# Scaling s by rows only in its two halves, with the row scales made for two tiles at once

## The chip, the cores and the metric

The kernel runs on one core of a Trainium2 chip. The metric is the time of one execution on the device in microseconds (us); lower is better. The core has five engines with a queue of instructions each, executed in order: PE multiplies matrices into PSUM, DVE (VectorE) does reductions and elementwise work, ACT (ScalarE) does functions and scaled copies, POOL (GpSimd) does elementwise work in SBUF, and SP issues the DMAs. They wait for each other by semaphores.

## The reference, cut to what matters

Two steps follow each other. The first is a causal attention over 7 taps with weights from a softmax over the taps; it turns `x` (8, 4160, 192) into 33280 rows of 192. The second works on these rows:

```python
h = x @ w_in                                   # 192 -> 1024
e = np.exp(h - max(h));  sm = e / (sum(e) + 1e-9)
solu = h * sm
ln = (solu - mean(solu)) / np.sqrt(var(solu) + 1e-6) * g_ln
return ln @ w_out                              # 1024 -> 192
```

max, sum, mean and var go over the 1024 columns of a row.

## The kernel before, in words

The 33280 rows lie as 128 partitions of 260 rows each. A *tile* t is one row of every partition, so there are 260 tiles of 128 rows, and tile after tile goes through the same stages.

*Attention, on POOL.* Four tiles make a group (the first two groups have two), 66 groups in all. `attention` multiplies x by the tap weights (L133), adds three taps to three (L139) and adds again into `half` (L141); `half` has two buffers. A reduction on DVE, the *final sum* (`last_sum`, L379, called `fin` in the order), makes the rows `a` of the group from it; `a` has three buffers. The tap weights come from a softmax in seven steps t0 to t6, for 16 tiles at once, spread over DVE, ACT and POOL.

*First product.* PE transposes two tiles of `a` (`xT`, L396). ACT takes the high part (L404); the low part comes from PE and ACT (L411, L418) or from DVE (L426, L427), taking turns by pairs. Ten matmuls make `h`, 128 x 1024, in PSUM (`mm1`, L440). There are three buffers `h`.

*Between the products*, by tile: DVE takes the negated maximum of a row (`max`, L454). Two small steps make the row scale: `bound` (`vb`, L458) takes the larger of |maximum| and 0.5, and `row_scale` (`vr`, L463) its reciprocal, SIGMA. ACT makes e = exp(h - max) and its row sum Z (`exp`, L467). DVE overwrites h with h x SIGMA x e and sums it (`solu`, L473). ACT sums the squares of its deviation (`sq`, L479). The result s is then split into two float16 numbers: the high half on ACT (`hi`, L486), with a scale of 2^14, and the low half, what is missing to it, on DVE (`lo`, L490). A DMA from SP transposes both (`tr`, L498).

*Second product.* 24 matmuls make `po` (`mm2`, L542), which has one buffer. ACT scales each row of it by OUT into `ot` (`out`, L553), and SP stores four tiles at once (`od`, L556).

*The statistics chain* (`scales`) makes OUT for four tiles at once from Z, SIGMA and the sums in eight steps f0 to f7, four small ones on ACT (L513, L517, L521 with L523, L529) and four reductions on DVE (all L510).

*The order.* Nothing is scheduled at run time: `issue_order` (L615) writes the order of every engine's queue before the program is built. It is a planner: each step has an engine, an assumed cost in ns and a list of steps that it follows; the engine that is free first takes, among its steps that are ready, the one with the smallest sum of tile number and an urgency from the table `URGENCY`. The assumed costs fix where steps of different engines come to stand relative to each other, thus also after which row maximum a final sum (which needs POOL) stands in DVE's queue.

Of the kernel before, what the change touches and what calls it, by code (L numbers as in the profile page):

```python
# [26 lines left out]
def tile_kernel(ctx: ExitStack, tc: tile.TileContext, x, weight_gen, w_in, w_out, g_ln, out):  # L27
    nc = tc.nc
    P = 128
# [14 lines left out]
    D2 = D - P  # L44
    FH = FF // 2

    const = ctx.enter_context(tc.tile_pool(name="const", bufs=1))
# [113 lines left out]
    nc.vector.memset(ones, 1.0 / FF)  # L161
    sq = const.tile([P, 4], F32, name="sq")

    minus = const.tile([P, 2, P], F32R, name="minus")
# [133 lines left out]
    def prepare_second(step, half=None):  # L298
# [11 lines left out]
        elif step == 6:  # L310
# [8 lines left out]
            )  # L319
            nc.vector.tensor_scalar_add(kinv, k, (127 - 73 + 1) << 23)  # L320
            nc.vector.tensor_scalar(k, k, -1, (127 + 73) << 23, op0=ALU.mult, op1=ALU.add)
        elif step == 4:
            k = second["k"] = small.tile([P, 1], F32, name="k", bufs=1)
            nc.scalar.copy(k, second["total"][:, 9:10])
            for n, factor in enumerate((-0.5, 1.5)):
                nc.scalar.activation(
                    newton[:, n : n + 1], second["total"][:, 10:11], AF.Copy, scale=factor
                )
        elif step == 7:
            js = slice(half * NJ // 2, (half + 1) * NJ // 2)  # L330
            nc.scalar.activation(
                w2_hl[:, js, 0, :], second["centred", half], AF.Copy, scale=second["k"]
            )
# [111 lines left out]

    ZE, SIGMA, Q, E, Y, V, Y2, R, OUT, M, Z, U, L, T, NMAX, HALF, BOUND = range(17)
    stats = const.tile([P, 6, TG, 17], F32, name="stats")
    nc.gpsimd.memset(stats[:, :, :, HALF], 0.5)
# [7 lines left out]

    def bound(t):
        nc.vector.tensor_reduce(  # L458
            stat(t, BOUND), stat(t, NMAX, 2), axis=AX.X, op=ALU.max, apply_absolute_value=True
        )  # L460

    def row_scale(t):
        nc.vector.reciprocal(stat(t, SIGMA), stat(t, BOUND))  # L463

# [6 lines left out]
    def solu(t):  # L471
        h, e = h_of[t], e_of[t]
        nc.vector.scalar_tensor_tensor(  # L473
            out=h, in0=h, scalar=stat(t, SIGMA), in1=e, op0=ALU.mult, op1=ALU.mult, accum_out=stat(t, M)
        )
# [8 lines left out]
    def high_half(t):  # L484
        hl = hl_of[t] = big.tile([P, 2, FF], F16, name="hl", bufs=3)
        nc.scalar.activation(hl[:, 0, :], h_of[t], AF.Copy, scale=2.0**14)  # L486

    def low_half(t):
        hl = hl_of[t]
        nc.vector.scalar_tensor_tensor(  # L490
            out=hl[:, 1, :], in0=h_of[t], scalar=2.0**14, in1=hl[:, 0, :],
            op0=ALU.mult, op1=ALU.subtract,
# [9 lines left out]
    def scales(t, step):  # L502
# [9 lines left out]
        if step == 0:  # L512
            nc.scalar.activation(of(ZE), of(Z), AF.Copy, bias=1e-9)  # L513
        elif step == 1:
            reduce(U, ZE, 2, ALU.mult)
        elif step == 2:
            nc.scalar.activation(of(E), of(U), AF.Square, scale=1e-3 * FF**1.5)  # L517
        elif step == 3:
            reduce(V, Q, 2, ALU.add)
        elif step == 4:  # L520
            nc.scalar.activation(of(L), of(V), AF.Ln)  # L521

            nc.scalar.activation(  # L523
                rows[:, :, Y : Y2 + 1 : 2], of(L).broadcast_to([P, n, 2]), AF.Exp, scale=-0.5
            )
        elif step == 5:
            reduce(T, Y, 3, ALU.mult)
        elif step == 6:
            nc.scalar.activation(  # L529
                of(R), of(T), AF.Identity, bias=newton[:, 1:2], scale=newton[:, :1]  # L530
            )
        elif step == 7:
            reduce(OUT, Y2, 2, ALU.mult)

# [52 lines left out]
    for n in range(LOADS):  # L587
        ops[f"lx{n}"] = at_chunk(load_x, n)
    for n in range(8):
        ops[f"f{n}"] = at(scales, n)  # L590
# [10 lines left out]
URGENCY = dict(  # L601
    a00=-20.7, a01=134, a02=5.2, a03=110.1, a04=63.2, a10=74.6, a11=-12, a12=-31.8, a13=49,
    a14=11.9, attA=47.9, attB=50.1, b0=42.1, b1=-15.1, b2=-35.2, b3=27.5, b4=95.3, b5=-24,
    c00=77.1, c01=-3.7, c02=-1.7, c10=81, c11=-48.9, c12=36.9, c20=-140.1, c21=-124.9, c22=47.5,
    c30=6.5, c31=125.3, c32=-83, dup=30.2, exp=67.3, f0=-40, f1=13.8, f2=-1.8, f3=0.8, f4=-12.5,
    f5=-133.2, f6=-27.2, f7=-17.9, fin=8.6, hi=4.9, lo=8.3, lw=8.7, lx0=-110.7, lx1=6.4, lx2=1.5,
    lx3=145.6, max=15.7, mm1=1.2, mm2=7.8, od=19.4, out=9, p30=99.5, p31=-21.1, p4=127.3,
    p5=-119.6, p6=38.8, p70=-21.5, p71=-29.7, p80=-68.4, p81=171.2, q00=149.9, q01=10.2, q02=126.8,
    q10=-10, q11=46.5, q12=-64.7, q20=-100.6, q21=-62, q22=138.4, q30=76.2, q31=-32, q32=-4,
    solu=-94.1, sq=153.2, t0=134, t1=-73, t2=29.5, t3=16, t4=-3.4, t5=130, t6=12.7, tr=-67.4,  # L610
    vb=-7.4, vr=-127.6, xT=-0.2, xhi=-140.5, xld=-4, xlo=-48.1, xn=-53.3,
)


def issue_order(run, starts, group, stat_group, loads):  # L615
# [37 lines left out]
    once("b5", SP, 0, "b4")  # L653
    for half in "01":
        once("p3" + half, DVE, 868, "q31", "mm1" if half == "0" else "q30", *(["p30"] if half == "1" else []))
    once("p5", PE, 220, "q02", "q12", "q22", "q32", "q31")
# [69 lines left out]
    for t in range(run):  # L726
        after = [("b5", 0), ("a04", 0), ("a14", 0)] if t == 0 else []
        if t < 3:

            after += ([("q10", 0), ("c30", 0)], [("p31", 0), ("sq", 0), ("lo", 0)], [("p80", 0)])[t]  # L730
        if t == 3:
            after.append(("p81", 0))
        add("mm1", t, PE, 2250, low_of(t), ("sq", t - 3), ("lo", t - 3), *after)
        add("max", t, DVE, 1131, ("mm1", t), ("exp", t - 4))
        add("vb", t, DVE, 70, ("max", t), ("f7", stats_of[t - 24] if t >= 24 else -1))
        add("vr", t, DVE, 70, ("vb", t))
        add("exp", t, ACT, 1091, ("max", t), ("sq", t - 2))
        add("solu", t, DVE, 1210, ("exp", t), ("vr", t))
        add("sq", t, ACT, 1091, ("solu", t))
        add("hi", t, ACT, 904, ("solu", t), ("tr", t - 3))  # L740
        add("lo", t, DVE, 1135, ("hi", t))
# [4 lines left out]
        else:  # L746
            after.append(("out", t - 1))
        add("mm2", t, PE, 2280, ("tr", t), *after)
        add("out", t, ACT, 304, ("mm2", t), ("f7", stats_of[t]), ("od", t // 4 * 4 - 5))
        if n := stat_group(t):  # L750
            tiles = range(t - n + 1, t + 1)
            add("f0", t, ACT, 200, *(("exp", u) for u in tiles))
            add("f1", t, DVE, 70, ("f0", t), *(("vr", u) for u in tiles))
            add("f2", t, ACT, 200, ("f1", t))
            add("f3", t, DVE, 70, ("f2", t), *(("sq", u) for u in tiles))
            add("f4", t, ACT, 400, ("f3", t))
            add("f5", t, DVE, 70, ("f4", t))
            add("f6", t, ACT, 200, ("f5", t), ("p4", 0))
            add("f7", t, DVE, 70, ("f6", t))
        if t % 4 == 3:  # L760
# [98 lines left out]
```

## Time and profile before

| what | before |
|---|---|
| median of 3 runs | 1400.43 us (1398.85 to 1400.59) |
| profiled execution | 1399.32 us |
| its span | 1397.5 us, so 1.8 us lie around it |
| mean granted clock of PE | 0.987 |
| HBM read, written | 46.19 MB, 25.56 MB |

The profile page gives each engine's busy time and its share of the span. A group of instructions is one line of the kernel on one engine: its name reads output<-inputs, then shapes, count, busy us, mean ns of one, and the idle time ahead of them with what ended it. A line of the waits reads: who, for whom, us in total, times, longest. In a line of the windows stand the stretch, its length, and then busy us and the count in brackets, for all five engines and PE's weight loads, or for those instructions alone that were asked for; the last three numbers are the granted clock, the DMA share and GB/s. A line of the timeline begins with its start and its duration in us.

### The profile page before, as it was taken

What the parts mean: (1) busy time and instruction counts of PE and PEld (TensorE: products, weight loads), DVE (VectorE), ACT (ScalarE), POOL (GpSimd) and SP (SyncE); (2) the same over time, 40 slices, a digit from 0 to 9 for tenths busy, and PEclk for the clock granted to TensorE, in tenths of its full rate; (3) what the DMA queues carried; (4) which work ended last, traced back from release to release, by engine and by line L of the source; (5) the groups of instructions that cost most, each with busy time, mean ns of one, the idle gap of its engine ahead of it and who ended that gap; (6) DMA issues with size and microseconds to landing.
All of it is one profiled execution on the core that took longest, in us unless ns stands there. A gap on an engine that the chain in (4) does not pass through costs nothing.

```text
span 1397.5 us, 25636 instructions
## 1 busy us (share of the span) xinstructions
PE 1252.0 (90%) x9508; PEld 1074.0 (77%) x9508; DVE 1249.2 (89%) x2135; ACT 1130.3 (81%) x2231; POOL 1247.8 (89%) x243
## 2 busy tenths in 40 slices
PE   0398999989999998989999999989999899999997
PEld 0277878878788787878888787878878788888786
DVE  2988999989999998899899999989999999999984
ACT  1577888878888887888788888878887888888885
POOL 1999999999999999999999999999999999998000
PEclk9999999999999999999999999999999999999999
DMA  3567769687878877786959777686969687656665
GB/s 94 168 146 177 152 131 200 135 182 129 184 129 173 168 145 159 132 203 123 199 111 191 142 149 171 131 183 125 209 112 207 117 184 144 129 118 129 128 123 121
DMA packets 565878, 211.43 MB, mean 151 GB/s; under 512 B 544457, under 2 KB 545913, under 8 KB 565752
## 3 DMA queue, kind: packets, MB, share of 16 engines
q1 hardware_dynamic: 565752, 209.78, 72.7%
q8 instruction: 75, 1.23, 0.4%
q14 instruction: 51, 0.42, 0.1%
HBM read 46.19 MB, written 25.56 MB: 51 GB/s over the span
## 4 chain that ended last, share of the span: by engine, by line
POOL 50%; DVE 18%; issue 13%; ACT 13%; PE 3%; DMA 2%; SPq 1%; POOLq 0%; DVEq 0%; ACTq 0%
POOL pr L133 26%; POOL pr L139 14%; POOL half L141 6%; DVE h L473 5%; ACT e L479 4%; ACT hl L486 4%; DVE stats L454 3%; DVE hl L490 3%; DVE a L379 2%; ACT e L467 2%; PE h L440 2%; POOL wt L114 2%; POOL wt L126 2%; DMA raw_a<-in_moe_w_in_dram 1%; PE po L542 1%
## 5 line engine op out<-in xcount | busy, mean ns | idle before, releaser
L133 POOL TENSOR_TENSOR pr<-xt,wt 128x5376 f32<-128x5376 f32 (+1 forms) x66 | 631.6, 9569 | 22.5 <-DMA xt<-zeros 19.8
L542 PE MATMUL po<-w_hl,hlT 128*128 128x192 f16 x6192 | 560.5, 248 | 27.7 <-ACT ot L553 26.8
L542 PEld LDWEIGHTS <-hlT 128*128 128x128 f16 x6240 | 519.0, 98 | 72.8 <-issue 70.0
L473 DVE SCALAR_TENSOR_TENSOR h<-h,stats,e 128x1024 f32<-128x1024 f32 x260 | 335.0, 1288 | 23.0 <-ACT e L467 11.2
L490 DVE SCALAR_TENSOR_TENSOR hl<-h,hl 128x1024 f16<-128x1024 f32 x260 | 316.8, 1220 | 34.0 <-ACT e L479 28.3
L486 ACT ACTIVATE hl<-h 128x1024 f16<-128x1024 f32 x260 | 267.5, 1029 | 96.5 <-DVE stats L510 53.2
L139 POOL TENSOR_TENSOR pr<-pr 128x2304 f32<-128x2304 f32 (+1 forms) x66 | 333.2, 5048 | 5.2
L454 DVE TENSOR_REDUCE stats<-h 128x1 f32<-128x1024 f32 x260 | 316.4, 1217 | 10.1 <-PE h L440 9.6
L467 ACT ACTIVATE e<-h,stats 128x1024 f32<-128x1024 f32 x260 | 292.7, 1126 | 34.2 <-DVE stats L454 30.0
L479 ACT ACTIVATE e<-h,stats 128x1024 f32<-128x1024 f32 x260 | 292.3, 1126 | 15.4 <-DVE hl L490 15.3
L440 PE MATMUL h<-wa_hi,x_hi 128*128 128x512 f32 x520 | 226.0, 435 | 40.2 <-ACT e L479 17.7
L141 POOL TENSOR_TENSOR half<-pr 128x1536 f32<-128x1536 f32 (+1 forms) x66 | 226.1, 3426 | 5.2
L440 PE MATMUL h<-wa_lo,x_hi 128*128 128x512 f32 x520 | 207.1, 398 | 0.0
L440 PE MATMUL h<-wa_hi,x_lo 128*128 128x512 f32 x520 | 206.6, 397 | 0.0
L440 PEld LDWEIGHTS h<-wa_hi,x_hi 128*128 128x128 f32 x520 | 99.3, 191 | 64.2 <-ACT e L479 23.2
L396 PE MATMUL pa<-ident,a 128*128 128x128 f32 x520 | 80.4, 277 | 46.4 <-DVE a L379 44.0
L379 DVE TENSOR_REDUCE a<-half 128x768 f32<-128x1536 f32 (+1 forms) x66 | 116.6, 1766 | 1.2 <-POOL half L141 1.2
L440 PEld LDWEIGHTS h<-wa_hi,x_lo 128*128 128x128 f32 x520 | 99.1, 191 | 23.3 <-ACT x_lo L418 0.2
L553 ACT ACTIVATE ot<-po,stats 128x192 f32<-128x192 f32 x258 | 111.0, 430 | 4.9 <-PE po L542 4.8
L396 PEld LDWEIGHTS pa<-ident,a 128*128 128x128 f32 x520 | 64.9, 143 | 62.3 <-DVE a L379 44.0
L440 PEld LDWEIGHTS h<-wa_lo,x_hi 128*128 128x128 f32 x520 | 99.8, 192 | 12.3
L440 PE MATMUL h<-wb_lo,x_lo 128*128 128x512 f32 x260 | 103.7, 399 | 0.0
(84 smaller groups left out, 1308.4 us busy)
## 6 DMA issues: line engine op xcount, KB each, us to landing
out_dram<-ot SPq DMA_DIRECT2D x65, 384.0 KB, 3.2
xt<-in_x_dram SPq DMA_DIRECT2D x30, 576.0 KB, 4.8
xt<-in_x_dram SPq DMA_DIRECT2D x30, 480.0 KB, 4.3
wt<-in_weight_gen_dram SPq DMA_DIRECT2D x15, 448.0 KB, 4.8
hlT<-hl SPq DMA_TRANSPOSE x260, 4.5
raw<-in_moe_w_out_dram SPq DMA_DIRECT2D x1, 1536.0 KB, 9.3
xt<-in_x_dram SPq DMA_DIRECT2D x3, 384.0 KB, 5.6
raw_a<-in_moe_w_in_dram SPq DMA_DIRECT2D x2, 512.0 KB, 11.4
```

What stands on the lines that cost most here:

```text
L133: nc.gpsimd.tensor_tensor(out=window(pr, 0, [(TG * D, K), (HG, n * H), (1, HG)]), in0=window(xt, t * D, [(D, K), (HG, n * H), (1, HG)]), i ...
L139: nc.gpsimd.tensor_tensor(out=pr[:, :3], in0=pr[:, :3], in1=pr[:, 3:6], op=ALU.add)
L141: nc.gpsimd.tensor_tensor(out=half, in0=window(pr, 0, [(2 * TG * D, 2), (D, n), (1, D)]), in1=window(pr, TG * D, [(5 * TG * D, 2), (D, n), ...
L396: nc.tensor.matmul(pa[:, n, i, :], a[:, (t + i) % TG, n * P : (n + 1) * P], ident, is_transpose=True, start=i == n == 0, stop=i == n == 1,)
L440: nc.tensor.matmul(h[:, fs], lhs, rhs[:, fs], start=n == 0, stop=n == len(terms) - 1)
L454: nc.vector.tensor_reduce(stat(t, NMAX), h_of[t], axis=AX.X, op=ALU.max, negate=True)
L467: nc.scalar.activation(e, h_of[t], AF.Exp, bias=stat(t, NMAX), accum_out=stat(t, Z))
L473: nc.vector.scalar_tensor_tensor(out=h, in0=h, scalar=stat(t, SIGMA), in1=e, op0=ALU.mult, op1=ALU.mult, accum_out=stat(t, M))
L479: nc.scalar.activation(e_of.pop(t), h_of[t], AF.Square, bias=stat(t, M), scale=-float(FF), accum_out=stat(t, Q),)
L486: nc.scalar.activation(hl[:, 0, :], h_of[t], AF.Copy, scale=2.0**14)
L490: nc.vector.scalar_tensor_tensor(out=hl[:, 1, :], in0=h_of[t], scalar=2.0**14, in1=hl[:, 0, :], op0=ALU.mult, op1=ALU.subtract,)
L542: nc.tensor.matmul(po[:, :D], hlT[:, half * NJ + j, :], w2_hl[:, j, w, :], start=n == 0, stop=n == len(terms) - 1,)
```

## The change

`solu` no longer multiplies by the row scale: it takes the constant 2^14 in its place, so it needs neither `vb` nor `vr`. The row scale SIGMA comes in where s is split: it replaces the constant 2^14 in `hi` and `lo`. `vb` and `vr` are done for two tiles at once, behind the maximum of the odd one, so that `hi` of an even tile follows the maximum of the next tile. The statistics chain drops SIGMA from its product of Z and SIGMA: six steps f0 to f5 are left, three on ACT (the first a square with a constant column `tiny` as its bias) and three on DVE, and the last of them multiplies SIGMA in. Constants (`UNIT`) keep the numbers in range.

In the planner the costs of the two products change from 2250 and 2280 to 2450 and 2200, a few steps of the start have other predecessors, and every urgency is new. The softmax steps of four chunks change places with groups in POOL's queue among the groups before tile 36; from there on POOL's queue is the same.

```diff
     def bound(t):
+        rows = stats[:, t // TG % 6, t % TG - 1 : t % TG + 1, :]
         nc.vector.tensor_reduce(
-            stat(t, BOUND), stat(t, NMAX, 2), axis=AX.X, op=ALU.max, apply_absolute_value=True
+            rows[:, :, BOUND], rows[:, :, NMAX : HALF + 1], axis=AX.X, op=ALU.max,
+            apply_absolute_value=True,
         )
     def row_scale(t):
-        nc.vector.reciprocal(stat(t, SIGMA), stat(t, BOUND))
+        rows = stats[:, t // TG % 6, t % TG - 1 : t % TG + 1, :]
+        nc.vector.reciprocal(rows[:, :, SIGMA], rows[:, :, BOUND])
...
     def solu(t):
-            out=h, in0=h, scalar=stat(t, SIGMA), in1=e, op0=ALU.mult, op1=ALU.mult, accum_out=stat(t, M)
+            out=h, in0=h, scalar=S_UNIT, in1=e, op0=ALU.mult, op1=ALU.mult, accum_out=stat(t, M)
...
-        nc.scalar.activation(hl[:, 0, :], h_of[t], AF.Copy, scale=2.0**14)
+        nc.scalar.activation(hl[:, 0, :], h_of[t], AF.Copy, scale=stat(t, SIGMA))
...
-            out=hl[:, 1, :], in0=h_of[t], scalar=2.0**14, in1=hl[:, 0, :],
+            out=hl[:, 1, :], in0=h_of[t], scalar=stat(t, SIGMA), in1=hl[:, 0, :],
...
         if step == 0:
-            nc.scalar.activation(of(ZE), of(Z), AF.Copy, bias=1e-9)
+            nc.scalar.activation(of(E), of(Z), AF.Square, bias=tiny, scale=1e-3 * UNIT)
         elif step == 1:
-            reduce(U, ZE, 2, ALU.mult)
-        elif step == 2:
-            nc.scalar.activation(of(E), of(U), AF.Square, scale=1e-3 * FF**1.5)
-        elif step == 3:
             reduce(V, Q, 2, ALU.add)
...
-            reduce(OUT, Y2, 2, ALU.mult)
+            reduce(OUT, Y2, 3, ALU.mult)
...
 URGENCY = dict(
-    a00=-20.7, a01=134, a02=5.2, a03=110.1, a04=63.2, a10=74.6, a11=-12, a12=-31.8, a13=49,
+    a00=-72.1, a01=-8.5, a02=6.8, a03=10.7, a04=5.4, a10=158.8, a11=116.1, a12=5.7, a13=11.5,
...
-        add("mm1", t, PE, 2250, low_of(t), ("sq", t - 3), ("lo", t - 3), *after)
+        add("mm1", t, PE, 2450, low_of(t), ("sq", t - 3), ("lo", t - 3), *after)
...
-        add("vb", t, DVE, 70, ("max", t), ("f7", stats_of[t - 24] if t >= 24 else -1))
-        add("vr", t, DVE, 70, ("vb", t))
+        if t % 2:
+            add("vb", t, DVE, 70, ("max", t), ("max", t - 1), ("f5", stats_of[t - 24] if t >= 24 else -1))
+            add("vr", t, DVE, 70, ("vb", t))
...
-        add("solu", t, DVE, 1210, ("exp", t), ("vr", t))
+        add("solu", t, DVE, 1210, ("exp", t))
-        add("hi", t, ACT, 904, ("solu", t), ("tr", t - 3))
+        add("hi", t, ACT, 904, ("solu", t), ("vr", t | 1), ("tr", t - 3))
...
-        add("mm2", t, PE, 2280, ("tr", t), *after)
+        add("mm2", t, PE, 2200, ("tr", t), *after)
```

First place: DVE's queue around the 45th final sum, that of tiles 172 to 175 (`a`<-`half`). Before, `h_9914` belongs to tile 162 and `h_9988` to tile 163 (L454 is the maximum, L473 the product, L490 the low half, L458 and L463 the row scale):

```order
L454 TENSOR_REDUCE stats_131<-h_9914 128x1
L458 TENSOR_REDUCE stats_131<-stats_131 128x1
L463 RECIPROCAL stats_131<-stats_131 128x1
L490 SCALAR_TENSOR_TENSOR hl_9936<-h_9863,hl_9936 128x1024
L379 TENSOR_REDUCE a_9984<-half_9761 128x4x192
L473 SCALAR_TENSOR_TENSOR h_9914,stats_131<-h_9914,stats_131,e_9975 128x1024
L454 TENSOR_REDUCE stats_131<-h_9988 128x1
```

In the changed kernel, whose lines have other numbers (L459 maximum, L481 product, L498 low half, L464 and L471 the row scale, L384 the final sum), `h_9456` belongs to tile 158 and `h_9523` to tile 159:

```order
L459 TENSOR_REDUCE stats_133<-h_9456 128x1
L498 SCALAR_TENSOR_TENSOR hl_9475<-h_9403,stats_133,hl_9475 128x1024
L481 SCALAR_TENSOR_TENSOR h_9456,stats_133<-h_9456,e_9515 128x1024
L384 TENSOR_REDUCE a_9539<-half_9304 128x4x192
L459 TENSOR_REDUCE stats_133<-h_9523 128x1
L431 TENSOR_TENSOR x_lo_9571<-pa_9518,x_hi_9567 128x256
L432 TENSOR_TENSOR x_hi_9567<-pa_9518,x_hi_9567 64x256
L464 TENSOR_REDUCE stats_133<-stats_133 128x2
L471 RECIPROCAL stats_133<-stats_133 128x2
```

The same final sum stands behind the maximum of tile 162 before (163 maxima ahead of it) and behind that of tile 158 now (159 ahead). At the 29th final sum (tiles 108 to 111) it is 102 and 99, at the last (256 to 259) 245 and 243. The row scale stands once behind the maximum of an odd tile.

Second place: ACT's queue at tiles 250 and 251. Before (L467 exponential, L486 high half, L479 squares, L553 scaled output), `h_15160` is tile 250 and `h_15222` tile 251:

```order
L486 ACTIVATE hl_15237<-h_15160 128x1024
L479 ACTIVATE e_15212,stats_131<-h_15160,stats_131 128x1024
L467 ACTIVATE e_15267,stats_131<-h_15222,stats_131 128x1024
L553 ACTIVATE ot_15235<-po_15239,stats_131 128x192
L513 ACTIVATE stats_131<-stats_131 128x4
L486 ACTIVATE hl_15288<-h_15222 128x1024
```

In the changed kernel (L475 exponential, L494 high half, L487 squares, L557 scaled output) `h_14817` is tile 250 and `h_14878` tile 251:

```order
L487 ACTIVATE e_14872,stats_133<-h_14817,stats_133 128x1024
L409 CAST x_hi_14917<-pa_14838 128x512
L475 ACTIVATE e_14922,stats_133<-h_14878,stats_133 128x1024
L557 ACTIVATE ot_14828<-po_14891,stats_133 128x192
L494 ACTIVATE hl_14933<-h_14817,stats_133 128x1024
L521 ACTIVATE stats_133<-stats_133,tiny_100 128x4
L494 ACTIVATE hl_14948<-h_14878,stats_133 128x1024
```

The high half of tile 250 stood ahead of its squares and of the exponential of tile 251; now it stands behind both, and the high halves of the two tiles follow each other.

More of the change, by code (lines that the diff above doesn't have):

```diff
@@ L443, in first_product @@
         h_of[t] = h
-    ZE, SIGMA, Q, E, Y, V, Y2, R, OUT, M, Z, U, L, T, NMAX, HALF, BOUND = range(17)
-    stats = const.tile([P, 6, TG, 17], F32, name="stats")
+    Q, E, Y, V, Y2, R, BOUND, OUT, M, Z, L, T, NMAX, HALF, SIGMA = range(15)
+    stats = const.tile([P, 6, TG, 15], F32, name="stats")
     nc.gpsimd.memset(stats[:, :, :, HALF], 0.5)
@@ L588, in tile_kernel @@
         ops[f"lx{n}"] = at_chunk(load_x, n)
-    for n in range(8):
+    for n in range(6):
         ops[f"f{n}"] = at(scales, n)
@@ L653, in issue_order @@
     once("b5", SP, 0, "b4")
-    for half in "01":
-        once("p3" + half, DVE, 868, "q31", "mm1" if half == "0" else "q30", *(["p30"] if half == "1" else []))
+    add("p30", 0, DVE, 868, ("q31", 0), ("mm1", 1))
+    once("p31", DVE, 868, "p30", "sq", "lo")
     once("p5", PE, 220, "q02", "q12", "q22", "q32", "q31")
@@ L752, in issue_order @@
             add("f0", t, ACT, 200, *(("exp", u) for u in tiles))
[L753 to L759, printed above, removed]
+            add("f1", t, DVE, 70, ("f0", t), *(("sq", u) for u in tiles))
+            add("f2", t, ACT, 400, ("f1", t))
+            add("f3", t, DVE, 70, ("f2", t))
+            add("f4", t, ACT, 200, ("f3", t), ("p4", 0))
+            add("f5", t, DVE, 70, ("f4", t), *(("vr", u | 1) for u in tiles))
         if t % 4 == 3:
```

45 lines of the change are left out of this document (24 added, 21 removed).

## Prediction

> **What bounds the kernel now.** I read the page first, for who is busy; then the busy time by stretches, then the waits; and last I counted instructions at chosen moments, because no share told enough.
>
> ```profile
> PE 1252.0 (90%) x9508; PEld 1074.0 (77%) x9508; DVE 1249.2 (89%) x2135; ACT 1130.3 (81%) x2231; POOL 1247.8 (89%) x243
> ```
>
>
> Three engines are near 90% of the span. By stretches (length, then busy us and count of PE, PEld, DVE, ACT, POOL) they differ:
>
> ```profile
> 1000.00:1200.00 200.00, 187.84 (x1441) 161.66 (x1439) 184.48 (x315) 168.41 (x333) 197.80 (x37) 0.99 0.76 151
> 1306.00:1376.00 70.00, 66.54 (x516) 57.28 (x516) 59.96 (x107) 56.76 (x112) 0.00 (x0) 1.00 0.62 126
> ```
>
> In the middle POOL is busy 98.9% (197.80 of 200), PE 94%, DVE 92%, ACT 84%. POOL hardly ever waits:
>
> ```profile
> POOL pr L133 <- DMA xt<-zeros: 19.8, 1, 19.8
> POOL wt L126 <- DVE wy L124: 7.0, 1, 7.0
> ```
>
> Those are its two large waits, one time each, before the first group is under way. So POOL walks through its 66 groups of tiles at its own pace and the main loop (product, maximum, exponential, product on DVE, halves, second product) follows. POOL's steps, with the end of the 45th group (tiles 172 to 175) and of the last (256 to 259):
>
> ```profile
> 886.58 3.45 POOL L141 TENSOR_TENSOR half<-pr 128x1536 f32<-128x1536 f32 x1
> 1285.77 3.46 POOL L141 TENSOR_TENSOR half<-pr 128x1536 f32<-128x1536 f32 x1
> ```
>
> They end at 886.58 + 3.45 = 890.03 and 1285.77 + 3.46 = 1289.23. How far is the main loop then? I counted POOL's last steps (L141, one a group, first fence) and the row maxima (L454 on DVE, one a tile, second fence) that had begun by such moments, the count in brackets:
>
> ```profile
> 0.00:580.60 580.60, 97.55 (x29) 0.98 0.73 154
> 0.00:890.00 890.00, 153.02 (x45) 0.98 0.75 155
> ```
>
> ```profile
> 0.00:580.60 580.60, 124.01 (x102) 0.98 0.73 154
> 0.00:890.00 890.00, 198.27 (x163) 0.98 0.75 155
> 0.00:1289.20 1289.20, 294.46 (x242) 0.99 0.74 153
> 890.00:1289.20 399.20, 96.19 (x79) 0.99 0.73 149
> ```
>
> 163 maxima by 890.0 and 242 by 1289.2: 79 in 399.2 us, a pace of 5.05 us a tile. The run ends 1397.5 - 1289.2 = 108.3 us after POOL does, with 18 maxima still to come. So the end is set by the main loop, which has fallen far behind POOL, and not by POOL itself.
>
> The place where the two meet is the final sum of a group (L379, on DVE), which reads what POOL wrote:
>
> ```profile
> L379 DVE TENSOR_REDUCE a<-half 128x768 f32<-128x1536 f32 (+1 forms) x66 | 116.6, 1766 | 1.2 <-POOL half L141 1.2
> ```
>
> DVE waited for POOL there 1.2 us in the whole run: before, each of these sums stands in DVE's order just behind the moment at which POOL is ready.
>
> **The change part by part: the order.** This is the largest term, and no line of the new arithmetic shows it. The planner's costs and urgencies are new, and so is the place of L379 among the maxima. In the listing of the kernel before, 163 maxima stand ahead of the 45th final sum; in the changed one 159. DVE executes in order, so in the changed kernel the 160th maximum can't begin before POOL has ended that group. POOL's own order and work are the same from tile 36 on (softmax steps change places among the groups before; that sum is the same), so this moment stays 890.0, where the kernel before was at 163. Everything behind the waiting sum on DVE is held: the next product, maximum and low half; behind them ACT (exponential, halves) and PE, which needs an h buffer back. The changed kernel is thus four tiles, at 5.05 us some 20 us, later at this point, whatever its engines could do. It is no single accident: ahead of the 29th final sum, whose group POOL ended at 580.6, stand 99 maxima, against the 102 that had begun.
>
> From there it has to catch up. The last final sum stands behind 243 maxima (245 before), so at 1289.2 it can have begun 243 at most, one more than before. That takes 84 tiles in 399.2 us, 4.75 us each. Slower than that, POOL no longer holds it and its own pace decides:
>
> maxima begun at 1289.2 = 159 + 399.2 / pace; time lost = (242 - that number) x pace; given back in the last 18 tiles = 18 x (5.05 - pace).
>
> **The change part by part: the pace.** DVE loses work:
>
> ```profile
> L463 DVE RECIPROCAL stats<-stats 128x1 f32<-128x1 f32 x260 | 41.7, 161 | 5.7
> L458 DVE TENSOR_REDUCE stats<-stats 128x1 f32<-128x2 f32 x260 | 38.3, 147 | 2.2
> L510 DVE TENSOR_REDUCE stats<-stats 128x4 f32<-128x8 f32 (+3 forms) x268 | 42.1, 157 | 13.4 <-ACT e L479 7.9 <-ACT stats L529 4.5 <-ACT stats L523 0.7
> L473 DVE SCALAR_TENSOR_TENSOR h<-h,stats,e 128x1024 f32<-128x1024 f32 x260 | 335.0, 1288 | 23.0 <-ACT e L467 11.2 <-ACT x_lo L418 0.5 <-ACT ot L553 0.5
> L490 DVE SCALAR_TENSOR_TENSOR hl<-h,hl 128x1024 f16<-128x1024 f32 x260 | 316.8, 1220 | 34.0 <-ACT e L479 28.3 <-ACT hl L486 3.8 <-ACT k L324 0.7
> ```
>
> Bound and reciprocal once for two tiles: 130 x (147 + 161) = 40.0 us less; two elements in place of one cost at most what L510 shows for four (157), so no more than 1.3 us comes back. The chain's four reductions become three: 67 x 157 = 10.5 us. Together some 50 us, 0.19 us a tile. The product (L473) loses its per-row operand and the low half (L490) gains one; if that is the 68 ns between their rows, the two cancel.
>
> ACT gains and loses:
>
> ```profile
> L486 ACT ACTIVATE hl<-h 128x1024 f16<-128x1024 f32 x260 | 267.5, 1029 | 96.5 <-DVE stats L510 53.2 <-DVE h L473 40.7 <-DVE stats L458 1.1
> L467 ACT ACTIVATE e<-h,stats 128x1024 f32<-128x1024 f32 x260 | 292.7, 1126 | 34.2 <-DVE stats L454 30.0 <-DVE stats L463 1.8 <-DVE stats L510 1.0
> L331 ACT ACTIVATE w_hl<-h,k 128x768 f16<-128x768 f32 x2 | 1.7, 897 | 0.0
> L513 ACT ACTIVATE stats<-stats 128x4 f32<-128x4 f32 (+1 forms) x67 | 15.9, 237 | 0.5
> L517 ACT ACTIVATE stats<-stats 128x4 f32<-128x4 f32 (+1 forms) x67 | 14.1, 211 | 1.9 <-DVE stats L510 1.8
> ```
>
> The high half now scales by a row's number. L467, as wide and with a per-row bias, is 97 ns longer than L486. L331 has a per-row scale on 768 columns: between L517 (211 at 4) and L486 (1029 at 1024) a plain one would take about 824, so the operand costs 73. 260 x (73 to 97) = 19 to 25 us more; L513 goes, 15.9 us less; the square gains a per-row bias, 67 x (0 to 97) = 0 to 6.5 us. Net 3 to 16 us, 0.01 to 0.06 us a tile, on an engine that is idle 16% of the time and waits 96.5 us ahead of this very step: nothing, while DVE is later than ACT. If that cover goes, it is 0.06.
>
> The change adds a wait: the high half of an even tile now needs the maximum of the next one, since their scales are made together. Queued behind it on ACT stand the partner's high half and its squares; DVE's low half waits for it, and PE for the h buffer. In ACT's new order it stands behind the partner's exponential, which needs the same maximum, so I cost it at nothing; if the three h buffers are too few for that, the pace suffers (a rival below). On SP the x loads stand four transposes earlier than before in the middle of the run; with the main loop four tiles later the moment is the same, so nothing.
>
> How much of DVE's 0.19 reaches the pace? Bounds: all of it, 4.86; or nothing, 5.05, if PE sets it. What PE waits for:
>
> ```profile
> PE po L542 <- ACT ot L553: 26.8, 39, 3.2
> PE pa L411 <- ACT x_hi L404: 19.9, 24, 3.5
> PE h L440 <- ACT e L479: 17.7, 19, 3.2
> ```
>
> Its largest waits in the loop are for ACT; these three make 64 us. And the stretch 1306 to 1376 is an experiment that the trace made itself: no final sums, no softmax, POOL silent, DVE down to 86% (59.96 of 70). The maxima there:
>
> ```profile
> L454 DVE TENSOR_REDUCE stats<-h 128x1 f32<-128x1024 f32 x14 | 17.1, 1219 | 1.2 <-PE h L440 1.2
> ```
>
> 14 in 70 us, 5.0 each: DVE was freed of 116.6 / 260 = 0.45 us a tile and the pace gained 0.05, with PE at 95%. By this row 0.19 would bring some 0.02; the other end is 0.19. PE is busy 94% of 5.05, or 4.74; each step below 5.05 must come out of its 0.31 of idle time. I take 0.10, in the middle, since PE's waits for ACT hang on the order too, and that is new everywhere: pace 4.95. Then 159 + 399.2 / 4.95 = 239.65; lost 2.35 x 4.95 = 11.6; given back 18 x 0.10 = 1.8. Span 1397.5 + 11.6 - 1.8 = 1407.3. The profiled execution took 1399.3 for its span of 1397.5, so 1.8 lies around it; it is 1.1 under the median of 1400.4. Forecast: 1409 us, slower.
>
> One page weighs the engines otherwise. The Trainium skill (Perfetto Trace Analysis, Identifying the Most-Contended Engine) holds that matmul busy time is a bad measure of PE and that its weight loads should be read in its place. In the stretch from 1000 to 1200 these are 161.66 of 200, 81%, under DVE's 92%; by that rule DVE limits the loop and its whole 0.19 comes off. The stretch after 1306 speaks against it: there PE's weight loads are 57.28 of 70, 82%, DVE is less busy, and the pace hardly moved.
>
> **The rivals.**
> *DVE is the limit* (beside it, that page's rule). Pace 4.86: 159 + 82.1 = 241.1; lost 0.9 x 4.86 = 4.4, given back 18 x 0.19 = 3.4; span 1398.5, time 1400: no change. For it: ACT's long waits ahead of L486 are all for DVE. Against: the stretch above. 0.12.
>
> *POOL holds it to the end: faster.* The new order loses fewer PE waits than I think, and the pace reaches POOL's 4.75: 243 at 1289.2, one tile ahead (4.75), and 18 x 0.30 = 5.4 in the rest: span 1387.3, time 1389. No pace gives more than about this, since the last final sum can't come sooner. The turn lies at 4.85, where loss and gift are equal; faster by 0.2% from 4.84 down, where PE would be busy 98% by its row. For it: PE's waits for ACT come from who stands ahead of whom, and a better order could take them all. 0.29 for all that is faster.
>
> *The pair wait binds.* Even tiles hold an h buffer until the partner's maximum is made; pace 5.10 rather than 4.95: 237.3, lost 24.0, and 0.9 more in the rest: time 1424. Against: ACT's idle time. 0.10.
>
> My forecast has 0.49; its own range runs from pace 4.89 (240.6; 6.8 lost, 2.9 back; 1403) to 5.05 (238; 20.2 lost; 1419.5).
>
> **How the numbers follow.** Time 1409. 0.2%, about what a measurement of this kernel can tell from no change, is 2.8 us: 1397.6 to 1403.2. Slower 0.49 + 0.10 = 0.59; same 0.12; faster 0.29. The range goes from POOL's floor, 1389, to the unchanged pace, 1419; left out are most of the pair case and a little below the floor.
>
> **What would show it.** Right: 159 maxima begun by 890.0 and 99 by 580.6; a wait of DVE for POOL ahead of the final sum of far more than 1.2 us, most of it before 900, and little after; POOL's last step still ending near 1289; then a pace of about 4.95. Bound and reciprocal counted 130 times, the high half at 1.10 to 1.13 us. Wrong: POOL ending much earlier, or 163 maxima at 890.0 (the order doesn't hold it), or a pace of 4.75 up to the end.

## The result, and the profile after

The changed kernel takes 1421.08 us (median of 4 runs, 1420.44 to 1421.65), the kernel before 1399.91 on the same chip (4 runs, 1398.85 to 1400.59). The ratio is 1.0152, with a 95% interval of 1.0134 to 1.0169: slower by some 21 us. The profiled execution took 1421.65, its span 1419.3; before it was 1397.5, so the spans differ by 21.8.

The page's busy line, after:

```profile
PE 1250.8 (88%) x9508; PEld 1065.5 (75%) x9508; DVE 1237.1 (87%) x1809; ACT 1152.5 (81%) x2164; POOL 1248.5 (88%) x243
```

All shares are lower than before or the same. PE and POOL do the same work in a longer time, DVE has 12.1 us less to do (1249.2 before), ACT 22.2 more (1130.3). An engine that had become the limit would stand nearer to 100%; none does. So something waits.

The count of row maxima (now L459 on DVE), in brackets, at the moments of the prediction:

```profile
0.00:580.60 580.60, 119.14 (x98) 0.97 0.70 150
0.00:890.00 890.00, 192.07 (x158) 0.98 0.71 152
0.00:1085.00 1085.00, 237.06 (x195) 0.98 0.72 154
0.00:1289.20 1289.20, 287.06 (x236) 0.98 0.72 151
890.00:1289.20 399.20, 94.99 (x78) 0.99 0.73 149
```

98 and 158: not above the 99 and 159 that the order of the final sums allows. But after 890 it goes on losing: 78 tiles in 399.2 us, 5.12 us each, where the forecast had 4.95. And DVE doesn't wait at the final sum (idle time ahead of it in the last column):

```profile
L384 DVE TENSOR_REDUCE a<-half 128x768 f32<-128x1536 f32 (+1 forms) x66 | 116.6, 1766 | 0.0
```

The wait was forecast there, and there is none. The list of waits names another place where ACT and DVE stand still behind POOL (us in total, times, longest):

```profile
ACT wt L121 <- POOL wt L117: 30.1, 13, 3.5
DVE wm L123 <- ACT wt L121: 23.1, 12, 3.1
```

These are steps of the taps' softmax: t1 on POOL (L117), t2, its exponential, on ACT (L121), t3, a sum, on DVE (L123). They come once for 16 tiles. One of them in the timeline (start, duration, in brackets the idle time before it and what ended it):

```profile
618.52 1.77 POOL L117 TENSOR_TENSOR wt<-wt,wm 128x896 f32<-128x896 f32 x1
620.33 0.95 ACT L121 ACTIVATE wt<-wt 128x896 f32<-128x896 f32 x1 [1.74 <-POOL wt L117]
621.31 1.09 DVE L123 TENSOR_REDUCE wm<-wt 128x128 f32<-128x896 f32 x1 [1.40 <-ACT wt L121]
```

t1 ends at 620.29, t2 starts at 620.33, and t3 follows it. The last time is the same:

```profile
1081.48 0.25 ACT L487 ACTIVATION_READ_ACCUMULATOR e<-h,stats 128x1 f32 x1
1084.82 0.95 ACT L121 ACTIVATE wt<-wt 128x896 f32<-128x896 f32 x1 [3.09 <-POOL wt L117]
1085.68 1.10 ACT L475 ACTIVATE e<-h,stats 128x1024 f32<-128x1024 f32 x1
```

ACT has nothing to do for 3.09 us, although exponentials of tiles are queued behind t2, and the row maximum that the next of them needs had ended on DVE at 1081.59 (L459, from 1080.38). So the loop can't be further at t2 than ACT's order has it, and POOL, which comes to t1 at its own pace, sets the time. How far that is, by the tile exponentials begun (two records each, so half the number in brackets): after (L475), at two of the t2,

```profile
0.00:620.33 620.33, 128.11 (x212) 0.98 0.71 153
0.00:1084.80 1084.80, 234.43 (x388) 0.98 0.72 154
```

and before (L467), at the same two:

```profile
0.00:619.40 619.40, 132.16 (x218) 0.98 0.74 156
0.00:1083.70 1083.70, 242.61 (x400) 0.99 0.75 157
```

After: 106 and 194, so 88 tiles in 464.5 us, 5.28 us each. Before: 109 and 200, 91 in 464.3, 5.10 each. The kernel before was held in the same place; its waits had shown it, with 31.4 us:

```profile
ACT wt L118 <- POOL wt L114: 31.4, 15, 4.3
```

The order before held it on a faster line. Behind the last t2 the loop is free: 62 maxima begin in the 300 us from 1090 to 1390, 4.84 us each (before, 57 in the 280 us from 1090 to 1370, 4.91), and in the stretch in which POOL is silent PE is busy 69.28 of 70 us:

```profile
1328.00:1398.00 70.00, 69.28 (x543) 59.52 (x543) 61.25 (x94) 62.13 (x117) 0.00 (x0) 1.00 0.68 130
```

The maxima by 1085, and those from 1090 to 1370, of the kernel before:

```profile
0.00:1085.00 1085.00, 244.54 (x201) 0.99 0.75 157
1090.00:1370.00 280.00, 69.42 (x57) 1.00 0.68 135
```

And from 1090 to 1390 of the changed one:

```profile
1090.00:1390.00 300.00, 74.69 (x62) 1.00 0.69 134
```

The account by the spans: 195 against 201 are six tiles fewer at 1085, at 4.84 us some 29; the other 59 go 0.07 faster each, some 4; 29 - 4 = 25, against 21.8 measured. Counts at one moment are good to about a tile, which is the rest.

The steps of the arithmetic, after:

```profile
L494 ACT ACTIVATE hl<-h,stats 128x1024 f16<-128x1024 f32 x260 | 291.1, 1124 | 8.5 <-DVE stats L471 4.4
L498 DVE SCALAR_TENSOR_TENSOR hl<-h,stats,hl 128x1024 f16<-128x1024 f32 x260 | 332.8, 1280 | 15.6 <-ACT e L487 9.0
L481 DVE SCALAR_TENSOR_TENSOR h<-h,e 128x1024 f32<-128x1024 f32 x260 | 319.5, 1229 | 62.1 <-ACT e L475 56.1
L518 DVE TENSOR_REDUCE stats<-stats 128x4 f32<-128x12 f32 (+3 forms) x201 | 32.1, 160 | 10.5 <-ACT stats L533 6.9 <-ACT e L487 3.1
L471 DVE RECIPROCAL stats<-stats 128x2 f32<-128x2 f32 x130 | 21.5, 166 | 3.8
L464 DVE TENSOR_REDUCE stats<-stats 128x2 f32<-128x4 f32 x130 | 20.2, 156 | 2.6
L521 ACT ACTIVATE stats<-stats,tiny 128x4 f32<-128x4 f32 (+1 forms) x67 | 20.7, 309 | 0.1
```

The high half went from 1029 to 1124 ns, the low half from 1220 to 1280, the product from 1288 to 1229, the square in the chain from 211 to 309. The small steps of DVE (L458, L463, L510 before) went from 122.1 to 73.8 us.

### The profile page after: what moved, and what is told of

The parts are those of the page before. It is cut to its first block, busy times and chain, and to the rows that moved or that the text cites. A ratio compares the mean times of both kernels' runs of the same rounds, so it can differ in the third digit from the quotient of the medians.

```text
span 1419.3 us, 24978 instructions
## 1 busy us (share of the span) xinstructions
PE 1250.8 (88%) x9508; PEld 1065.5 (75%) x9508; DVE 1237.1 (87%) x1809; ACT 1152.5 (81%) x2164; POOL 1248.5 (88%) x243
## 4 chain that ended last, share of the span: by engine, by line
POOL 60%; DVE 13%; ACT 11%; issue 10%; DMA 2%; PE 2%; SPq 0%; POOLq 0%; ACTq 0%; DVEq 0%
POOL pr L136 32%; POOL pr L142 17%; POOL half L144 7%; DVE hl L498 6%; ACT e L487 4%; ACT hl L494 3%; ACT e L475 3%; DVE h L481 2%; DVE a L384 2%; DVE stats L459 2%; POOL wt L117 2%; DMA xt<-in_x_dram 2%; POOL wt L129 2%; PE h L445 1%; PE po L546 1%
## 5 line engine op out<-in xcount | busy, mean ns | idle before, releaser
L481 DVE SCALAR_TENSOR_TENSOR h<-h,e 128x1024 f32<-128x1024 f32 x260 | 319.5, 1229 | 62.1 <-ACT e L475 56.1
L487 ACT ACTIVATE e<-h,stats 128x1024 f32<-128x1024 f32 x260 | 292.4, 1125 | 82.3 <-DVE h L481 45.5
L498 DVE SCALAR_TENSOR_TENSOR hl<-h,stats,hl 128x1024 f16<-128x1024 f32 x260 | 332.8, 1280 | 15.6 <-ACT e L487 9.0
L459 DVE TENSOR_REDUCE stats<-h 128x1 f32<-128x1024 f32 x260 | 316.4, 1217 | 18.0 <-PE h L445 17.8
L475 ACT ACTIVATE e<-h,stats 128x1024 f32<-128x1024 f32 x260 | 290.9, 1119 | 35.7 <-DVE stats L459 34.5
L494 ACT ACTIVATE hl<-h,stats 128x1024 f16<-128x1024 f32 x260 | 291.1, 1124 | 8.5 <-DVE stats L471 4.4
L401 PE MATMUL pa<-ident,a 128*128 128x128 f32 x520 | 83.8, 282 | 82.2 <-DVE a L384 47.2
L401 PEld LDWEIGHTS pa<-ident,a 128*128 128x128 f32 x520 | 59.0, 142 | 110.3 <-DVE a L384 46.3
L384 DVE TENSOR_REDUCE a<-half 128x768 f32<-128x1536 f32 (+1 forms) x66 | 116.6, 1766 | 0.0
L445 PEld LDWEIGHTS h<-wa_hi,x_lo 128*128 128x128 f32 x520 | 98.9, 190 | 22.8
L557 ACT ACTIVATE ot<-po,stats 128x192 f32<-128x192 f32 x258 | 108.4, 420 | 8.5 <-PE po L546 8.2
L445 PE MATMUL h<-wb_hi,x_lo 128*128 128x512 f32 x260 | 103.2, 397 | 0.0
```

Of the source, the lines that this page charges most:

```text
L384: nc.vector.tensor_reduce(columns(t)[:, :, :D], half.rearrange("p j t d -> p t d j"), axis=AX.X, op=ALU.add)
L445: nc.tensor.matmul(h[:, fs], lhs, rhs[:, fs], start=n == 0, stop=n == len(terms) - 1)
L459: nc.vector.tensor_reduce(stat(t, NMAX), h_of[t], axis=AX.X, op=ALU.max, negate=True)
L475: nc.scalar.activation(e, h_of[t], AF.Exp, bias=stat(t, NMAX), accum_out=stat(t, Z))
L481: nc.vector.scalar_tensor_tensor(out=h, in0=h, scalar=S_UNIT, in1=e, op0=ALU.mult, op1=ALU.mult, accum_out=stat(t, M))
L487: nc.scalar.activation(e_of.pop(t), h_of[t], AF.Square, bias=stat(t, M), scale=-float(FF), accum_out=stat(t, Q),)
```

## The experiments

Theory A: the new order holds the loop at t2, and the new arithmetic costs little. Theory B: the new arithmetic (above all the row scale in the halves) sets the pace, and the waits for POOL are a by-product. All kernels were timed beside the kernel before, which gave 1400.0, 1399.8 and 1400.1 in the three sets of runs, so times of different sets are compared directly. "Interval" is that of the ratio to it, at 95%.

**The product costs of the planner.** These two numbers are part of the change and touch no arithmetic. In the changed kernel they are set back:

```diff
-        add("mm1", t, PE, 2450, ...
+        add("mm1", t, PE, 2250, ...
-        add("mm2", t, PE, 2200, ("tr", t), *after)
+        add("mm2", t, PE, 2280, ("tr", t), *after)
```

> The changed kernel with the planner's old costs for the two products (2250 and 2280), its arithmetic and its urgencies kept. Theory A (the order holds the main loop: ACT's softmax exponential t2 stands behind too few tile exponentials and waits there for POOL's t1, which ends the last time near 1085 us): the last t2 stands behind 198 tile exponentials, not 194, so 4 tiles x 4.8 us = 19 us come off 1421: 1402. Theory B (the new arithmetic itself, the pair wait and the longer high half, sets the pace): no change, 1421.

1408.06 us, ratio 1.0059, interval 1.0042 to 1.0075. 13 of the 21 us are gone with the same arithmetic, so B alone falls; A expected 19. The hold is weaker, not gone:

```profile
ACT wt L121 <- POOL wt L117: 24.3, 13, 4.7
```

The reverse, the new costs in the kernel before:

> The kernel before with the planner's new costs for the two products (2450 and 2200), its arithmetic and urgencies kept. Theory A: the last t2 stands behind 194 tile exponentials in place of 200, so 6 tiles x 4.9 us = 29 us are added to 1400: 1429, though nothing of the arithmetic is changed. Theory B: 1400.

1442.52 us, ratio 1.0303 (1.0288 to 1.0319): with the old arithmetic, two numbers of the planner cost 42 us. A's sign, but more than A's 29. Here POOL is stopped too, by half buffers that DVE empties late:

```profile
ACT wt L118 <- POOL wt L114: 27.6, 12, 4.3
POOL half L141 <- DVE stats L510: 10.4, 3, 3.6
POOL half L141 <- DVE a L379: 9.9, 6, 2.1
```

By the maxima begun, the loss has two parts. At 1085 there are 194 in place of the 201 before:

```profile
0.00:1085.00 1085.00, 235.34 (x194) 0.98 0.72 152
```

Seven tiles at 4.91 us are some 34. Behind the last t2, from 1090 to 1370, 55 begin in place of 57, some 10 us more. Most of POOL's stops at `half` lie in this second part, and its last step ends at 1311.8 in place of 1289.2. That the stops are what costs these 10 us wasn't tried apart.

**A planner that thinks POOL slower.** If POOL's steps cost more in the planner's book, more tiles are put ahead of each t2 and each final sum. Nothing else changes; POOL's real work is the same. For a factor s:

```diff
-        costs = (wide, 13 * n, 190 + 6 * n, wide, 190 + n, 60 + 8.4 * n, 13 * n)
+        costs = (wide, 13 * s * n, 190 + 6 * n, wide, 190 + n, 60 + 8.4 * n, 13 * s * n)
-        add("attA", t, POOL, 14206 if full else 7302, ...
+        add("attA", t, POOL, 14206 * s if full else 7302 * s, ...
-        add("attB", t, POOL, 3380 if full else 1764, ...
+        add("attB", t, POOL, 3380 * s if full else 1764 * s, ...
```

The changed kernel with s = 1.08:

> The changed kernel with POOL's assumed costs 8% higher in the planner and nothing else. Theory A: the last t2 stands behind 208 tile exponentials (194 in the changed kernel), so ACT and DVE no longer wait for POOL's softmax steps; up to 14 tiles x 4.8 us = 67 us come off, 1354, or less where the loop's own pace with the softmax steps in it, not seen so far, is slower than 4.9 us a tile: 1354 to 1385. Theory B: 1421.

1402.35 us (10 runs, 1400.30 to 1409.64), ratio 1.0026 (1.0011 to 1.004). 19 us better than the changed kernel, but not the time below 1385 that A wanted. The hold at t2 is down to 3.9 us; in its place POOL now waits for DVE.

```profile
POOL wt L117 <- DVE stats L464: 21.4, 9, 3.6
POOL wt L129 <- DVE wy L127: 11.8, 3, 6.9
ACT wt L121 <- POOL wt L117: 3.9, 3, 2.0
```

The last t2 starts at 1131.8, 47 us later than in the changed kernel (1084.8). That takes back most of the 68 us that 14 more tiles at 4.84 us are worth. A factor of 1.08 goes too far for this kernel, as 1.04 below shows. The kernel before with s = 1.05:

> The kernel before with POOL's assumed costs 5% higher in the planner and nothing else. Theory A: the kernel before is held in the same way, the last t2 stands behind 207 tile exponentials in place of 200, so up to 7 x 4.9 = 34 us come off 1400: 1366 to 1390. Theory B says nothing of a hold: 1400. Beside the third run it also shows what the new arithmetic is worth where the order does not hold it: a pace shorter by some 0.1 us a tile would make that one faster by up to 25 us.

1390.68 us, ratio 0.9934 (0.992 to 0.9949): the kernel before was held as well, by some 9 us. Its wait at t2 is down from 31.4 us:

```profile
ACT wt L118 <- POOL wt L114: 4.8, 2, 3.4
```

The sign is A's in both kernels; the time is just above A's range, whose upper end is 1390.

The changed kernel with s = 1.04:

> The changed kernel with POOL's assumed costs 4% higher in the planner. The last t2 stands behind 202 tile exponentials (194 in the changed kernel, 208 at 8%). Theory A: between the two, the hold costs 8 tiles less: 1421 - 8 x 4.8 = 1383 if the own pace allows it; with the own pace of 5.0 seen at 8%, about 1395 (1390 to 1402), and less waiting of POOL than at 8%.

1398.49 us (10 runs, 1397.56 to 1400.70), ratio 0.9992 (0.9982 to 1.0002): inside what was expected, 3 us over its middle. With s = 1.04 and the old product costs as well:

> The changed arithmetic and urgencies with the old costs of the two products and POOL's assumed costs 4% higher. The last t2 stands behind 204 tile exponentials, 205 to 207 being the count that gave 1391 with the old arithmetic. Theory A: 1385 to 1395, better than the kernel before. Theory B (the new arithmetic costs time by itself): over 1400.

1391.62 us, ratio 0.994 (0.9925 to 0.9955), inside A's range; the hold is gone:

```profile
ACT wt L121 <- POOL wt L117: 0.2, 1, 0.2
```

The arithmetic of the change is all in it, and the time is that of the kernel before with a relaxed order (1390.68) within 1 us. The kernel before with s = 1.04:

> The kernel before with POOL's costs 4% higher. The last t2 stands behind fewer tile exponentials than at 5% (207), more than before (200). If less release than 5% leaves POOL fewer waits, as 4% against 8% did with the changed arithmetic: 1386 to 1391; if the hold comes back: 1391 to 1396.

1395.45 us (6 runs), ratio 0.9968 (0.9956 to 0.998), inside the second range: the hold is back in part (7.9 us of waits at t2, against 4.8 at 5% and 31.4 before).

**The hold at t2 taken out by itself.** In the changed kernel's finished order, POOL does t1 one group earlier, so that its result is there when ACT comes to t2. The two steps that feed it (t0, and the load of the weights) move ahead with it, and the weights get a fourth buffer. Nothing else moves; the final sums keep their places.

```diff
-        wt = ws[c] = io.tile([P, TC * HK], F32, name="wt", bufs=3)
+        wt = ws[c] = io.tile([P, TC * HK], F32, name="wt", bufs=4)
+    for c in starts[5:-1]:
+        i = order.index(("t1", c))
+        order.pop(i)
+        while order[i - 1][0] != "attA":
+            i -= 1
+        order.insert(i - 1, ("t1", c))
...
```

> The changed kernel with POOL's softmax step t1 of each chunk one group of tiles earlier in POOL's queue (and its DVE step t0 five maxima earlier, its load earlier, with a fourth buffer wt so that this is possible); every other place in every queue kept, the final sums' too. ACT's t2 should then find t1 done. If the final sums hold the loop next, as the prediction had it: DVE waits for POOL at them, 5 us or more in sum (0.0 in the changed kernel), 159 maxima begun by 890 at most, and the time 1409 to 1416. If t2 alone held it: no waits at the final sums, own pace from the start, 1404 or less.

1409.68 us, ratio 1.0071 (1.0056 to 1.0086). Now DVE waits for POOL at the final sum, 12 times:

```profile
DVE a L384 <- POOL half L144: 14.1, 12, 3.2
ACT wt L121 <- POOL wt L117: 1.1, 1, 1.1
```

and the maxima begun:

```profile
0.00:890.00 890.00, 193.43 (x159) 0.99 0.72 153
0.00:1289.20 1289.20, 290.16 (x239) 0.99 0.73 152
```

159 and 239 where the prediction had 159 and 239.65, and its time of 1409. The two holds lie one behind the other; t2's is the stricter one, and costs 1421.1 - 1409.7 = 11.4 us more.

**The price of the row scale in the halves.** The next three stand on the changed kernel with s = 1.08 (1402.35), so that the order is the same. They leave the row scale out of one half or both, so they give prices of single steps and are no kernels to use. First both halves with a constant:

```diff
-        nc.scalar.activation(hl[:, 0, :], h_of[t], AF.Copy, scale=stat(t, SIGMA))
+        nc.scalar.activation(hl[:, 0, :], h_of[t], AF.Copy, scale=2.0**-3)
-            out=hl[:, 1, :], in0=h_of[t], scalar=stat(t, SIGMA), in1=hl[:, 0, :],
+            out=hl[:, 1, :], in0=h_of[t], scalar=2.0**-3, in1=hl[:, 0, :],
```

> The run with POOL's assumed costs 8% higher (1402 us, its pace 5.0 us a tile with nearly no waits for POOL's softmax steps), with a constant in place of the row scale in both halves, so that the rows are left unscaled there: the high half loses its per-row operand (some 95 ns of ACT) and its wait for the pair's reciprocal; the order of all queues is the same. Theory B (the pair wait and the longer high half set the own pace): 0.1 us a tile or more, 1376 or less. Theory C (they lie beside the path; the own pace comes from PE and the order): 1402, within 4.

1385.65 us, ratio 0.9896 (0.9882 to 0.9911): 16.7 us less. Neither theory's number; B has a part. Two things left together, the length of the operand and the wait for the partner's maximum. The next one has a column of constants, which is as long to read and waits for nothing:

```diff
+    eighth = const.tile([P, 1], F32, name="eighth")
+    nc.vector.memset(eighth, 2.0**-3)
-        nc.scalar.activation(hl[:, 0, :], h_of[t], AF.Copy, scale=stat(t, SIGMA))
+        nc.scalar.activation(hl[:, 0, :], h_of[t], AF.Copy, scale=eighth)
...
```

> The run with POOL's costs 8% higher (1402 us) with a constant column (one number a row, always 1/8) in place of the row scale in both halves, so that rows are left unscaled: the per-row operand stays, the wait for the pair's reciprocal goes. The run with a plain constant took 1386. If the operand's length (95 ns on ACT, 60 ns on DVE a tile) costs those 17 us: 1402. If the pair wait does: 1386. Between: both.

1400.68 us (10 runs, 1398.36 to 1403.79), ratio 1.0007 (0.9997 to 1.0016). The halves are as long as with SIGMA:

```profile
L496 ACT ACTIVATE hl<-h,eighth 128x1024 f16<-128x1024 f32 x260 | 291.1, 1123 | 4.6 <-DVE h L483 3.6
L500 DVE SCALAR_TENSOR_TENSOR hl<-h,eighth,hl 128x1024 f16<-128x1024 f32 x260 | 332.7, 1281 | 22.5 <-ACT e L489 14.3 <-ACT hl L496 6.3
```

So the length is 15.0 of the 16.7 us; 1.7 are left for the pair wait, no more than the spread of these ten runs. Then the high half alone with a plain constant, the low half as in the change:

> The same run (1402 us) with a plain constant in the high half alone; the low half keeps the row scale, so that the two do not fit each other. If ACT's longer high half and its wait are the price: 1386 as with a constant in both. If DVE's longer low half is: 1402.

1393.56 us, ratio 0.9955 (0.994 to 0.997): 8.8 us less than with SIGMA, and 7.9 more than with no row scale in either half; between the two times expected. ACT's row in it:

```profile
L494 ACT ACTIVATE hl<-h 128x1024 f16<-128x1024 f32 x260 | 266.9, 1029 | 7.7 <-DVE h L481 4.7
```

ACT's 95 ns are worth some 8.8 us, DVE's 60 ns some 7.9. The 1402.35 under the first is a median of ten runs that spread over 9 us, so the split is good to a us or two.

**What DVE's relief is worth.** The kernel before with s = 1.05 (1390.68), without bound and reciprocal, and with a constant in the product:

```diff
+    nc.gpsimd.memset(stats[:, :, :, SIGMA], 2.0**-3)
-            out=h, in0=h, scalar=stat(t, SIGMA), in1=e, op0=ALU.mult, ...
+            out=h, in0=h, scalar=2.0**-3, in1=e, op0=ALU.mult, ...
-        max=maximum, vb=bound, vr=row_scale, ...
+        max=maximum, vb=lambda t: None, vr=lambda t: None, ...
```

> The kernel before with POOL's costs 5% higher (1391 us) and without bound and reciprocal: a constant 1/8 stands for the row scale, in the product too, so rows are left unscaled. DVE loses 308 ns of short instructions a tile and the product its per-row operand (60 ns), with no new operand anywhere. If DVE's relief reaches the pace in full: 0.25 us a tile or more, 1330. By the prediction's half: 0.1 to 0.15, 1355 to 1365. If it lies beside the path: 1386 to 1391.

1362.93 us, ratio 0.9738 (0.9722 to 0.9755): 27.8 us less, 0.107 us a tile, inside the range "by the prediction's half". The busy lines, first with these steps, then without:

```profile
PE 1246.5 (90%) x9508; PEld 1066.6 (77%) x9508; DVE 1247.1 (90%) x2135; ACT 1129.7 (81%) x2231; POOL 1249.0 (90%) x243
```

```profile
PE 1244.5 (91%) x9508; PEld 1067.2 (78%) x9508; DVE 1184.6 (87%) x1615; ACT 1126.5 (83%) x2231; POOL 1248.2 (92%) x244
```

By the rows of the kernel before, 95 us went (41.7 + 38.3 for the two steps, 260 x 59 ns = 15 in the product), but DVE's busy time falls by 62.5: a part of a small step overlaps its neighbours on DVE. Of the 62.5, 44% reaches the time. DVE's relief may be worth more than that, since POOL holds this run again in part. The waits at t2 are 9.1 us, where they were 4.8, and POOL is busy 198.04 us of the 200 from 600 to 800:

```profile
ACT wt L118 <- POOL wt L114: 9.1, 6, 3.5
600.00:800.00 200.00, 192.25 (x1479) 164.83 (x1478) 180.87 (x244) 173.04 (x341) 198.04 (x38) 0.99 0.79 166
```

## Why the prediction was right and wrong

**The order decides: right.** With the new arithmetic and a relaxed order the time is 1391.6, with the old arithmetic 1390.7. With the shipped orders they are 1421.1 and 1399.9. So the shipped order costs 29.5 us in the changed kernel and 9.2 before; of the difference of 21.2 us, 20.3 are order, 0.9 arithmetic, as far as the two relaxed orders are equally good. The prices of the single steps, each taken in another order, come out as small: 12.1 us less on DVE at 44% are 5 gained, ACT's high half is 8.8 lost.

**The caps at 580.6 and 890.0: right as caps.** 98 and 158 maxima had begun, against 99 and 159. That they came so near isn't the caps' doing: no final sum waited, and t2 held the loop.

**"The place where the two meet is the final sum of a group": the step that failed.** It was a place where they meet, the second strictest. The strictest was t2 on ACT, which reads what POOL's t1 wrote. The prediction looked at what DVE reads from POOL, and counted only the order of the final sums; it put the softmax steps aside, since the sum of POOL's work was unchanged. The row for it (31.4 us, 15 times) stood in the waits of the kernel before, and the prediction made nothing of it. The "wait of DVE for POOL ahead of the final sum of far more than 1.2 us" was 0.0. With t2 freed, the wait, the 159, the 239 and the 1409 all came as forecast; so the mechanism was computed rightly for a hold that another one hid. That even the time came out within 1 us is in part luck, since the pace in that sum was put together from two wrong terms, as follows.

**"The unchanged pace", 5.05, less 0.10: two terms wrong.** Half of the stretch over which 5.05 was counted (890 to 1289.2) lies ahead of the last t2, where t2 held the kernel before: 38 maxima in the 195 us from 890 to 1085, 5.13 each. Behind it that kernel went at 4.91 with nothing changed. The row that was to show how little DVE's relief brings (14 maxima in 70 us, 5.0 each) can't tell 4.7 from 5.4, a maximum more or less. And the 0.10 gained isn't borne out: with both orders relaxed the new arithmetic is 0.9 us slower, not 26 faster.

**"From there … Slower than that, POOL no longer holds it": wrong with it.** t2 holds the loop up to 1084.8. At 1289.2, 236 maxima had begun rather than 239.65: 3.65 tiles at 4.95 are 18 us; some 6 came back behind. That makes the 12 us between the forecast span, 1407.3, and 1419.3. Of the 6, 24 tiles at 4.84 rather than 4.95 are 2.6; the rest is less than one tile, and counts tell no more.

**DVE's relief: a term mis-sized.** By the rows some 50 us were to go, and 48.3 went (122.1 - 73.8). The busy time fell by 12.1 only. The prediction added durations of small steps as though each stood alone; DVE's groups before already summed to 1383 us, against 1249.2 busy. That some half of a relief reaches the pace is what the run without bound and reciprocal shows (44%); but here there were 0.05 us a tile to halve, not 0.19.

**The high half at nothing: mis-sized.** Its length was forecast well (1.10 to 1.13; 1124 ns) and cover was claimed because ACT waited for DVE ahead of it. It cost 8.8 us. The wait of 96.5 us ahead of it was a sum over the run, not room in every tile; that the low half and PE get their data later where there is none is the likely way, but the runs show only the price. The fallback that the prediction named, 0.06 us a tile, would be 16 us; the run gives 0.034. The Trainium skill (ScalarE: Activation LUTs, section What ACT_TABLE_LOAD costs) has 93 ns for each per-row operand of such an instruction; the trace agrees, with 95 here and 98 on the square.

**Operands on DVE cancel: right in size.** -59 and +60 ns.

**The rivals.** "The pair wait binds" gave a time of 1424, near the result, by another cause: the column of constants leaves 1.7 us for it, within the spread. "DVE is the limit" (the rule of the Trainium skill, Perfetto Trace Analysis, Identifying the Most-Contended Engine) is half borne out: 62.5 us off DVE gave 27.8, but 24 us off ACT's high half (290.6 to 266.9), on an engine idle 13% of the time in the middle of the run with s = 1.08 (busy 173.40 of the 200 us from 1000 to 1200), gave 8.8. POOL, busier than DVE (98.9% in the middle before), is left out of that rival. "POOL holds it to the end" didn't come about: POOL's last step ends where it did, and the loop is behind it.

**Open:** why the kernel before with the new product costs loses 10 us behind the last t2 too; how much DVE's relief gives where POOL holds nothing; why the repeated runs with s = 1.08 spread over 9 us. The three longest of these (1406.59 to 1409.64) were granted a mean clock of 0.986 to 0.988, the four shortest (1400.30 to 1401.67) 0.994; which is the cause of which isn't shown.

## What to carry to other kernels

When queues are written out beforehand, list every instruction by which a fast loop reads from an engine that keeps its own pace, and count for each of them how much of the loop stands ahead of it: the strictest one decides, and its waits can be small (30 us in sum, 3.5 at most) while it holds the whole loop. A change that alters arithmetic and order together is judged apart: relax the order of both kernels first, then compare. Take the relief of an engine from its busy time, not from the sum of its instructions' durations.

## What the runs showed of the hardware that was not expected

- An operand of a number per row in place of a constant costs 95 ns on ACT (1029 to 1124 at 128x1024) and 60 ns on DVE (1220 to 1280), whether the column was just computed or constant (1123 and 1281).
- Small steps on DVE overlap their neighbours: removing 95 us of durations freed 62.5 us of DVE, and in the change 48.3 freed 12.1. The changed kernel's trace has it step by step: a reduction of the chain (L518) starts at 1076.28 and takes 0.17 us, and the bound (L464) starts at 1076.37.
- Of PE, DVE and ACT none is the limit by itself: they are busy 94%, 92% and 84% in the middle of the loop before, and each us taken off DVE or ACT gave part of a us. By DVE's busy time it was 0.44 (27.8 of 62.5); by the durations of the instructions 0.51 (7.9 of the low half's 15.4, 332.4 to 317.0) and 0.37 (8.8 of the high half's 24, ACT).
- Of the kernels that keep the row scale whole, the fastest is the kernel before with POOL's planned costs 5% higher, 1390.68 us (ratio 0.9934); the changed kernel with the old product costs and 4% on POOL's is level with it at 1391.62 (0.994). The reference has no row scale; it sets the size of the float16 halves, and OUT takes it out again. The kernel before with a constant in its place is the fastest of all (1362.93). For which inputs a constant would do is not shown.
